# Padding the SBUF tiles of a three-stage kernel so that every tile TensorE reads begins at a multiple of 128 bytes

## The chip, the cores and the metric

The kernel runs on one core of a Trainium2 chip. The metric is device time in microseconds (us) of that core, the median of several runs. The engines are TensorE (PE, with its weight loads listed apart as PEld), VectorE (DVE), ScalarE (ACT), GpSimd (POOL) and SyncE (SP, which issues most DMAs).

## What is computed

Three layers one after the other, all in fp32. B=2 batches, S=768 positions, H=8 heads of 64, so rows of 512 numbers.

```python
# 1: retention, state decays by gamma[h] per head
state = gamma * state + outer(k[t], v[t]);  y[t] = scale * q[t] @ state
# 2: mixture of 8 experts, one expert e per row (argmax of the gate, or held from the row before)
h = relu(x @ w1[e]);  x = softmax(x @ w_gate)[e] * (h @ w2[e])      # 512 -> 1024 -> 512
# 3: 4 causal attention experts, the two with the largest gate are added
q, k, v = x @ wq[e], x @ wk[e], x @ wv[e]
a = softmax(causal(scale * q @ k.T))
out += mask[e] * w[e] * (a @ v @ wo[e])
```

## The kernel before

**Precision.** A product in fp32 is made of several faster ones: each factor is split into a high part in the type fp32r (one ACT copy) and a rest (one DVE subtraction), and three products are added in PSUM: high by high, low by high, high by low (`terms`). So nearly every matmul comes three times, with names that end in h or l, or are called `whi`/`wlo` and `hh`/`hl`.

**Stage 1** (0 to about 68 us) works through chunks of 128 positions with the tiles of the pool `s1`, and routes the rows to experts. Two `clear` DMAs (L556) write zero rows from the tile `ZR` into `x2_d` (`x_d` in the trace), the buffer into which the experts later put their rows.

**Stage 2** (about 68 to 243 us) takes the experts one after the other, sorted by their number of rows N (`CAPS`). The 64 weight pieces of 512 KB (`fetch_piece`, from `in_w_dram` into `wraw`, 5 buffers in the pool `ring`) are split into `whi` (L196, ACT) and `wlo` (L202, DVE), 10 buffers each; `prepare` keeps the splits five pieces ahead. The first layer runs over four blocks f of 2 x 128 hidden columns: for N above 224 it takes 2 x 12 matmuls of N columns (L931; the weights are stationary, the rows of the expert, x0h/x0l or xx, are the moving operand). Otherwise it takes pairs, L943 with 2N columns and L945 with N columns. Each block goes into one of three PSUM banks "B"; hh (ACT, L932) and hl (DVE, L933) read the bank and so free it. hh and hl come from the pool `mx`, whose memory is that of `s1` after stage 1. The second layer (L978; L974 for small remainders) has 512 columns: hh or hl is stationary, whi or wlo the moving operand. An indirect DMA puts the rows into `x2_d` (L1000).

**Stage 3** (about 243 to 378 us) projects q and k (L1130, 12 matmuls of 256 columns; stationary wqh, wql, wkh, wkl, moving x0h/x0l or xh/xl in turn), v with the gate logits (L1168, 12 matmuls of 260 columns; stationary x, moving wvh/wvl), makes scores (L1239), softmax (L1252 DVE, L1262 ACT, L1273 POOL), transposes (L1295), values (L1315) and the output (L1336 and, for the last group, L1363; stationary oh/ol, moving woh/wol). A flag OV decides at the end whether a slow variant must run, which it does not here.

**Order.** In stages 1 and 2 the order of each engine is written out by hand; the framework adds the semaphore waits, and it adds one wherever a tile takes memory that an earlier tile still holds. Pools give out addresses in the order of the calls, so the size of one tile moves all that follow it. Where the tiles begin, in bytes modulo 128, per partition:

| tile | before | after |
|---|---|---|
| x0h, x0l, ID, WZ, at, oh, ol | 0 | 0 |
| whi, wlo | 96 | 0 |
| hh, hl | 64 | 0 |
| xx (rows of an expert; the low half of the larger uneven experts apart) | 64 | 0 |
| wqh, wql, wkh, wkl, woh, wol | 64 | 0 |
| wvh, wvl, their four rows | 64, 80, 96, 112 and 0, 16, 32, 48 | 0 |
| ks, qh, ql, vv, xh, xl | 64 | 0 |
| blq, blk, am (stage 1) | 64 | 0 |
| gate matrix IW, its four rows | 64, 100, 8, 44 | 0 |
| xg (rows gathered for an expert) | differ | differ |

Of the kernel before, what the change touches and what calls it, by code (L numbers as in the profile page):

```python
# [32 lines left out]
RW = DM + E  # L33
E2, HD = 4, 64
# [77 lines left out]
def kernel(  # L112
# [13 lines left out]
    nc = tc.nc  # L126

    cst = ctx.enter_context(tc.tile_pool(name="cst", bufs=1))
# [16 lines left out]
    PM = cst.tile([128, E, E], F32, name="PM")  # L145
    OD = cst.tile([1, E], I32, name="OD")
    TF = cst.tile([128, 2], F32, name="TF")
    ZR = cst.tile([128, RW], F32, name="ZR")
    SH = ZR[:, :2 * E].rearrange("p (i e) -> p i e", e=E)
    WZ = cst.tile([128, 128], BF16, name="WZ")  # L150
    ONES = cst.tile([128, 128], F32, name="ONES")
    IO = cst.tile([128, CAP], BF16, name="IO")
# [14 lines left out]
    raws, pieces, ords = {}, {}, []  # L167
# [6 lines left out]
    def fetch_piece(i):  # L174
        if i >= NP:
            return
        e, r = divmod(i, 8)
        raws[i] = ring.tile([128, 1040], F32, name="wraw", bufs=RAWS)[:, :1024]
        src = w1 if r < 4 else w2
        if e:  # L180
            if e > len(ords):
                n = slice(1, 2) if e == 1 else slice(2, E)
                ords.extend(nc.values_load_multi_w_load_instructions(
                    OD[0:1, n], engines=[mybir.EngineType.SP], min_val=0, max_val=E - 1)[1])
            src = src[bass.ds(ords[e - 1], 1), r % 4].rearrange("e p n -> (e p) n")
        else:
            src = src[e, r % 4]
        parts = 1 if e else 2
        for x in range(parts):
            n = slice(x * 1024 // parts, (x + 1) * 1024 // parts)  # L190
            nc.sync.dma_start(raws[i][:, n], src[:, n])
# [23 lines left out]
                in_offset=bass.IndirectOffsetOnAxis(ap=ix[:, i], axis=0), bounds_check=T * (RW // E), oob_is_err=False)  # L215

    def first_gather():
        zi = cst.tile([128, 1], I32, name="zi")
        zo = cst.tile([128, E], F32, name="zo")
        nc.gpsimd.memset(zi, 0)  # L220
        nc.gpsimd.indirect_dma_start(
            out=zo, out_offset=None, in_=drow.rearrange("t (k e) -> (t k) e", e=E),
            in_offset=bass.IndirectOffsetOnAxis(ap=zi, axis=0), bounds_check=3 * H * C // 2 // E - 1, oob_is_err=False)
# [28 lines left out]

    with tc.tile_pool(name="s1", bufs=2) as s1:
        XB, QT, KD, QD, AM, XR, XT, LL = {}, {}, {}, {}, {}, {}, {}, {}
        N1 = NC * B

        def load_half(n, x):
# [22 lines left out]
        load_half(2, 1)  # L280
        load_half(3, 1)
        IWN = 128 + E + 1
        IW = s1.tile([128, H // 2, IWN], F32, name="IW", bufs=1)
        DT = s1.tile([128, 2, H // 2, C], F32, name="DT", bufs=1)
        XRT = s1.tile([128, B, RW], F32, name="xr", bufs=1)
        nc.gpsimd.memset(XRT[:, :, :E], 0.0)
        SB = []
        for b in range(B):
            SB.append(s1.tile([128, H // 2, D], F32, name=f"SB{b}", bufs=1))
        DN = s1.tile([128, B, NC], F32, name="DN", bufs=1)  # L290
        pS = bank("B", [128, B, H // 2, D])
        pR = bank("B", [128, 512])
        pB = bank("B", [128, 512])
# [18 lines left out]
        pI = pB[:, 2 * E:2 * E + NC]  # L312
        pOne = pR[:, 384:]
        pW8, pU = pB[:, 64:64 + E], pB[:, 64 + E:64 + 2 * E]
        W8 = s1.tile([1, E], BF16, name="W8", bufs=1)
        nc.tensor.matmul(pOne, ONB[0:1], ONB[0:1], start=True, stop=True)

        PA = {}
# [514 lines left out]
    W3, W3R = {}, {}  # L833
    W3S = (("wq", wq, [128, 4, 256]), ("wk", wk, [128, 4, 256]), ("wv", wv, [128, 4, 260]), ("wo", wo, [128, 2, 512]))

    def fetch_w3(i):
        name, src, shape = W3S[i]
        n = shape[1] * shape[2]
        W3R[i] = ring.tile([128, 1040], F32, name="wraw", bufs=RAWS)
        nc.sync.dma_start(W3R[i][:, :n], src.rearrange("p a n -> p (a n)"))  # L840

    def split_w3(i):
        name, src, shape = W3S[i]
        n = shape[1] * shape[2]
        hi = w3.tile(shape, F32R, name=name + "h")
        lo = w3.tile(shape, F32R, name=name + "l")
        rr = W3R[i][:, :n].rearrange("p (a n) -> p a n", a=shape[1])
        nc.scalar.activation(hi, rr, AF.Copy)
        nc.vector.tensor_tensor(out=lo, in0=rr, in1=hi.bitcast(F32), op=OP.subtract)
        W3[name] = (hi, lo)  # L850

    with tc.tile_pool(name="mx", bufs=2) as mp:
# [5 lines left out]
        def turn2(e, i):  # L858
            if e >= E:
                return  # L860
            if i == 0:
                XX[e] = packed(mp.tile([128, 4 * 2 * CAP], F32R, name="xx"), CAPS[e], k=4)
                XH[e], XL[e] = XX[e][:, :, 0, :], XX[e][:, :, 1, :]
                PC[e] = mp.tile([128, 2, 1 + E], F32, name="pc")
            pT = bank("A", [128, 4, 128])
            for d in range(4):
                nc.tensor.transpose(pT[:, d, :], XG[e, i][:, E + d * 128:E + (d + 1) * 128], ident)  # L867
            w = min(CAPS[e] - i * 128, 128)
            r = slice(i * 128, i * 128 + w)
            nc.scalar.activation(XH[e][:, :, r], pT[:, :, :w], AF.Copy)  # L870
            nc.vector.tensor_tensor(out=XL[e][:, :, r], in0=pT[:, :, :w], in1=XH[e][:, :, r].bitcast(F32),
                                    op=OP.subtract)
            nc.vector.tensor_tensor_reduce(out=PC[e][:, i, 1:], in0=XG[e, i][:, :E], in1=PM[:, e], scale=1.0,
                                           scalar=0.0, op0=OP.mult, op1=OP.add, accum_out=PC[e][:, i, :1])
# [22 lines left out]
        done[:] = [9, 4]  # L897
        order = ExitStack()
        order.enter_context(tc.manual_schedule(engines={ENG.PE, ENG.DVE, ENG.Activation, ENG.Pool, ENG.SP}))
        for e in range(E):  # L900
            if e == 0:
                gather(1, None)
# [161 lines left out]
    def stage3(ready=None, midway=lambda: None):  # L1064
# [21 lines left out]

        def open_group(b, g):
            if g == 0:
                LG[b] = s3.tile([128, NC, E2], F32, name="lg")
            if (b * NG + g) % 2 == 0:  # L1090
                XH3[b, g], XL3[b, g] = X0
            else:
                XH3[b, g], XL3[b, g] = (s3.tile([128, 4, GW], F32R, name=n, bufs=1) for n in ("xh3", "xl3"))
            for e in range(E2):
                QH[b, g, e] = s3.tile([128, GW], F32R, name=f"qh{e}", bufs=3)
                QL[b, g, e] = s3.tile([128, GW], F32R, name=f"ql{e}", bufs=3)
                if g == 0:
                    KS[b, e] = s3.tile([128, S], F32R, name=f"ks{e}")
# [78 lines left out]

            return evac

        TR = s3.tile([128, E2, E2], F32, name="TR", bufs=1)  # L1180
        nc.vector.tensor_tensor(out=TR, in0=cn("w4")[:, None, :].to_broadcast([128, E2, E2]),
                                in1=cn("w4")[:, :, None].to_broadcast([128, E2, E2]), op=OP.is_gt)

        def gates(b, g):
            sh = [128, GB, E2]
            l = LG[b][:, g * GB:(g + 1) * GB]
            sq = sh + [E2]
            V = nc.vector
            m = s3.tile([128, 2, GB, 1], F32, name="gm")
            q = s3.tile([128, 2] + sq[1:], F32, name="gq")  # L1190
            f = s3.tile(sh, F32, name="gf")
            ex = s3.tile(sh, F32, name="ex3")
            wt = s3.tile(sh, F32, name="wt", bufs=4)
            mine = l[:, :, :, None].to_broadcast(sq)
            others = l[:, :, None, :].to_broadcast(sq)
            yield V.tensor_reduce(out=m[:, 0], in_=l, op=OP.max, axis=AX.X)
            yield V.tensor_tensor(out=ex, in0=l, in1=m[:, 0].to_broadcast(sh), op=OP.subtract)
            yield nc.scalar.activation(ex, ex, AF.Exp)
            yield V.tensor_tensor(out=q[:, 0], in0=others, in1=mine, op=OP.is_equal)
            yield V.tensor_tensor(out=q[:, 1], in0=q[:, 0], in1=TR[:, None].to_broadcast(sq), op=OP.mult)  # L1200
            yield V.tensor_tensor(out=q[:, 0], in0=others, in1=mine, op=OP.is_gt)
            yield V.tensor_reduce(out=f, in_=q.rearrange("p k i e o -> p i e k o"), op=OP.add, axis=AX.XY)
            yield V.tensor_scalar(f, f, 1.5, None, op0=OP.is_lt)
            yield V.tensor_tensor(out=ex, in0=ex, in1=f, op=OP.mult)
            yield V.tensor_reduce(out=m[:, 1], in_=ex, op=OP.add, axis=AX.X)
            yield V.tensor_scalar(m[:, 1], m[:, 1], 1e-9, None, op0=OP.add)
            yield V.reciprocal(m[:, 1], m[:, 1])
            yield V.tensor_tensor(out=wt, in0=ex, in1=m[:, 1].to_broadcast(sh), op=OP.mult)
            WT[b, g] = wt
# [484 lines left out]
```

## Time and profile before

| | us |
|---|---|
| median of 3 runs | 385.43 (383.79 to 387.71) |
| the profiled execution | 383.58 |
| its span in the trace | 382.1 |
| its mean granted TensorE clock | 0.998 of full speed |

The profiled execution is one run, 1.85 us under the median; 1.5 us of it lie outside the span. PE is listed as busy for 98% of the span, DVE for 72%, ACT for 61%. The ends of matmuls are modelled, so that the durations of neighbouring matmuls overlap in the trace (a listed duration is longer than the distance to the next start). How fast PE really goes through a row of matmuls is therefore read from the chain that ended last, whose pieces lie end to end: its length of a piece divided by its count.

### The profile page before, as it was taken

How to read it: one execution, taken by the hardware profiler on the slowest of the kernel's cores; microseconds unless marked ns; L12 is line 12 of the kernel's file. 1: busy time of each engine (PE TensorE's matmuls, PEld its weight loads, DVE VectorE, ACT ScalarE, POOL GpSimd, SP SyncE). 2: the span in 40 equal slices, each digit the busy share in tenths (PEclk: the TensorE clock that was granted, in tenths of full speed). 3: DMA queues.
4: the chain of work that ended last, by engine and by line, in shares of the span. 5: the costliest groups of instructions: out<-in, count | busy, mean ns of one | idle time of the engine just before them, and what ended most of it. 6: DMA issues, size and time to landing. Idle time of an engine off the chain costs nothing.

```text
span 382.1 us, 8618 instructions
## 1 busy us (share of the span) xinstructions
PE 374.5 (98%) x3035; PEld 328.1 (86%) x3035; DVE 276.8 (72%) x761; ACT 233.1 (61%) x549; POOL 128.6 (34%) x177
## 2 busy tenths in 40 slices
PE   8999998999999999999999999999999999999995
PEld 3899986988979798898989798899989988988774
DVE  4568877785766778688888993368886877669762
ACT  3455573464656756677787873367776765649641
POOL 1865462063305013131310011435545342424440
PEclk9999999999999999999999999999999999999999
DMA  7999995589675767767787772141012101001212
GB/s 215 398 320 329 308 370 193 158 266 344 215 261 173 244 215 249 274 216 249 242 256 242 255 270 70 51 139 57 5 52 57 28 2 50 7 30 27 57 41 77
DMA packets 27144, 66.99 MB, mean 175 GB/s; under 512 B 5061, under 2 KB 5445, under 8 KB 27096
## 3 DMA queue, kind: packets, MB, share of 16 engines
q1 hardware_dynamic: 24402, 58.82, 47.3%
q0 software_dynamic: 2544, 7.42, 5.6%
q8 instruction: 26, 0.43, 0.5%
q14 instruction: 22, 0.18, 0.1%
q10 hardware_dynamic: 150, 0.14, 0.1%
HBM read 55.77 MB, written 11.07 MB: 175 GB/s over the span
## 4 chain that ended last, share of the span: by engine, by line
PE 87%; DMA 8%; ACT 2%; issue 1%; DVE 1%; SPq 1%; POOL 0%; ACTq 0%; POOLq 0%; DVEq 0%
PE C L978 21%; PE B L931 9%; PE C L1130 8%; PE B L943 5%; PE C L1315 5%; PE B L1295 5%; PE A L1239 4%; DMA blk<-in_blk_dram 4%; PE C L1168 4%; PE C L1336 4%; PE A L943 3%; DMA x_d<-xr 3%; PE B L945 2%; PE C L974 2%; PE C L377 2%; PE A L867 2%
## 5 line engine op out<-in xcount | busy, mean ns | idle before, releaser
L202 DVE TENSOR_TENSOR wlo<-wraw,whi 128x1024 fp32r<-128x1024 f32 x62 | 74.4, 1222 | 14.6 <-ACT whi L196 14.6
L196 ACT ACTIVATE whi<-wraw 128x1024 fp32r<-128x1024 f32 x64 | 65.7, 1051 | 4.0 <-DMA wraw<-in_w_dram 4.0
L1000 POOL DMA_INDIRECT x_d<-y,SI x16 | 19.1, 1191 | 122.8 <-ACT y L990 78.3
L1273 POOL TENSOR_SCALAR a<-a,mx,wt 128x128 f32<-128x128 f32 (+5 forms) x48 | 34.0, 716 | 49.5 <-PE A L1239 14.4
L978 PE MATMUL C<-whi,hh 128*128 128x512 f32 (+4 forms) x112 | 45.4, 406 | 0.0
L1262 ACT ACTIVATE a<-a,mx 128x128 f32<-128x128 f32 (+5 forms) x48 | 32.1, 669 | 20.7 <-DVE mx L1252 19.1
L978 PE MATMUL C<-whi,hl 128*128 128x512 f32 (+4 forms) x112 | 44.3, 395 | 0.0
L978 PE MATMUL C<-wlo,hh 128*128 128x512 f32 (+4 forms) x112 | 44.2, 395 | 0.0
L943 PE MATMUL B<-xx,whi 128*128 128x384 f32 (+3 forms) x100 | 30.9, 363 | 0.0
L1252 DVE CUSTOM_DVE_ANT_0 a<-A,MR 128x384 f32<-128x384 f32 (+3 forms) x48 | 25.4, 530 | 1.9 <-PE A L1239 1.3
L1295 PE MATMUL B<-ID,a 128*128 128x128 f32 x168 | 26.0, 274 | 0.0
L945 PE MATMUL B<-xx,wlo 128*128 128x192 f32 (+3 forms) x100 | 25.6, 256 | 0.0
L978 PEld LDWEIGHTS C<-whi,hl 128*128 128x128 f32 (+4 forms) x112 | 20.0, 179 | 6.0
L978 PEld LDWEIGHTS C<-wlo,hh 128*128 128x128 f32 (+4 forms) x112 | 20.2, 180 | 5.1
L978 PEld LDWEIGHTS C<-whi,hh 128*128 128x128 f32 (+4 forms) x112 | 20.1, 179 | 4.7
L232 POOL DMA_INDIRECT xg<-x_d,GI x14 | 17.4, 1241 | 19.8 <-DMA wraw<-in_w_dram 15.9
L917 ACT ACTIVATE hh<-t 128x128 fp32r<-128x128 f32 (+4 forms) x56 | 16.3, 318 | 12.2 <-DVE t L949 12.0
L1295 PEld LDWEIGHTS B<-ID,a 128*128 128x128 f32 x168 | 19.8, 140 | 2.4 <-issue 0.9
L1239 PE MATMUL A<-ks,qh 128*128 128x256 f32 (+3 forms) x56 | 21.5, 384 | 0.0
L1315 PE MATMUL C<-at,vv 128*64 128x256 f32 (+1 forms) x204 | 20.6, 347 | 0.0
L943 PEld LDWEIGHTS B<-xx,whi 128*128 128x128 f32 x100 | 18.7, 187 | 0.6
L945 PEld LDWEIGHTS B<-xx,wlo 128*128 128x128 f32 x100 | 19.1, 191 | 0.2
(349 smaller groups left out, 970.9 us busy)
## 6 DMA issues: line engine op xcount, KB each, us to landing
wraw<-in_w_dram SPq DMA_DIRECT2D x56, 512.0 KB, 4.3
blq<-in_blk_dram SPq DMA_DIRECT2D x16, 256.0 KB, 6.8
blk<-in_blk_dram SPq DMA_DIRECT2D x16, 256.0 KB, 6.5
wraw<-in_w_dram SPq DMA_DIRECT2D x16, 256.0 KB, 5.3
x_d<-xr SPq DMA_DIRECT2D x12, 260.0 KB, 6.3
xr<-x_d SPq DMA_DIRECT2D x10, 256.0 KB, 2.6
blq<-in_blk_dram SPq DMA_DIRECT2D x4, 512.0 KB, 6.7
blk<-in_blk_dram SPq DMA_DIRECT2D x4, 512.0 KB, 9.6
```

What stands on the lines that cost most here:

```text
L196: nc.scalar.activation(hi, raws[i], AF.Copy)
L202: eng.tensor_tensor(out=lo[:, n], in0=raws[i][:, n], in1=hi[:, n].bitcast(F32), op=OP.subtract)
L931: nc.tensor.matmul(ph[:, a, :N], w[:, k, n], x[:, k, :N], start=m == 0, stop=m == 11)
L943: nc.tensor.matmul(pa, wh[:, k, n], XX[e][:, k], start=k == 0, stop=False, skip_group_check=True)
L945: nc.tensor.matmul(pa[:, 1], wl[:, k, n], XX[e][:, k, 0], start=False, stop=k == 3, skip_group_check=True)
L978: nc.tensor.matmul(pys[i][:rows], h[:, a, n], w[:, a, :], start=f == 0 and a == 0 and m == 0, stop=f == 3 and a == 1 and m == 2)
L1130: nc.tensor.matmul(pp, w[:, k, a * 128:(a + 1) * 128], x[:, k, :], start=m == 0, stop=m == 11)
L1239: nc.tensor.matmul(ps[:, :w], qq[b, g, e][:, tq], KS[b, e][:, s0:s0 + w], start=m == 0, stop=m == 1)
L1262: nc.scalar.activation(AA[u][:, :n], AA[u][:, :n], AF.Exp, bias=mx[:, 0, i:i + 1], scale=-1.0, accum_out=mx[:, 1, i:i + 1])
L1273: nc.gpsimd.tensor_scalar(a[:, :n], a[:, :n], mx[:, 1, i:i + 1], WT[b, g][:, i, e:e + 1], op0=OP.mult, op1=OP.mult)
L1295: nc.tensor.transpose(pT[:, s - s0, :], a[:, s * C:(s + 1) * C], ident)
L1315: nc.tensor.matmul(po[j * HD:(j + 1) * HD, r], VV[b, s][:, e * HD:(e + 1) * HD], at[j][:, s, r], start=s == 0, stop=s == ns - 1, skip_grou ...
```

## The change

No instruction is added, removed or made larger; one split (wv) is written as 128x4x260 instead of 128x1040. Tiles are padded or allocated in another order so that the table above results. `ZR` (the zero rows of the clears), which had its home in the pool of constants, and the two small tiles of `first_gather` move into the pool `s1`; `SH`, which shared ZR's memory, gets a tile of its own.

```diff
-    ZR = cst.tile([128, RW], F32, name="ZR")
-    SH = ZR[:, :2 * E].rearrange("p (i e) -> p i e", e=E)
+    SH = cst.tile([128, 2, E], F32, name="SH")
+    cst.tile([128, 120], F32, name="gap")
...
-        raws[i] = ring.tile([128, 1040], F32, name="wraw", bufs=RAWS)[:, :1024]
+        raws[i] = ring.tile([128, 1056], F32, name="wraw", bufs=RAWS)[:, :1024]
...
     def first_gather():
-        zi = cst.tile([128, 1], I32, name="zi")
-        zo = cst.tile([128, E], F32, name="zo")
+        zi = s1.tile([128, 1], I32, name="zi", bufs=1)
+        zo = s1.tile([128, E], F32, name="zo", bufs=1)
...
         XB, QT, KD, QD, AM, XR, XT, LL = {}, {}, {}, {}, {}, {}, {}, {}
+        ZR = s1.tile([128, 640], F32, name="ZR", bufs=1)[:, :RW]
...
-        IW = s1.tile([128, H // 2, IWN], F32, name="IW", bufs=1)
+        IW = s1.tile([128, H // 2, 160], F32, name="IW", bufs=1)[:, :, :IWN]
...
+    W3P = {n: 288 if n == "wv" else shape[2] for n, _, shape in W3S}
+    W3T = {n: [w3.tile([128, 2 if n == "wo" else 4, W3P[n]], F32R, name=n + x) for x in "hl"]
+           for n in ("wq", "wk", "wo", "wv")}
...
-        hi = w3.tile(shape, F32R, name=name + "h")
-        lo = w3.tile(shape, F32R, name=name + "l")
+        hi, lo = (t[:, :, :shape[2]] for t in W3T[name])
...
+        ring.tile([128, 88], F32, name="end", bufs=1)
```

The other lines pad XRT, DN, W8, pc, LG, TR and gm in the same way. The code after `before` L217 lies 1 to 5 lines further down (L932 becomes L937, L978 becomes L983).

The instructions stay in their order, save for a few; their waits don't. ACT at the start of stage 2, before (x0h and hh are the rows and hidden activations of the first expert, whi the high parts of weight pieces; the names in brackets are the semaphores, DMAHW those of DMA queues, DMASW that of GpSimd's DMAs):

```order
L779 ACTIVATE x0h<-C 128x512 [waits PE_49] x2
L196 ACTIVATE whi<-wraw 128x1024 [waits DMAHW2_49]
L932 ACTIVATE hh<-B 128x512 [waits DVE_49,DMAHW6_49,PE_49,DMAHW7_49,Activation_49,Pool_49]
L196 ACTIVATE whi<-wraw 128x1024 [waits DMAHW4_49,DMAHW3_49]
L932 ACTIVATE hh<-B 128x512 [waits PE_49]
```

And ACT at the same place, now:

```order
L780 ACTIVATE x0h<-C 128x512 [waits PE_49] x2
L196 ACTIVATE whi<-wraw 128x1024 [waits DMAHW2_49]
L1645 TENSOR_LOAD OV [waits DVE_49]
L937 ACTIVATE hh<-B 128x512 [waits DMAHW4_49,DMASW0_49,DMAHW5_49,DVE_49,DMAHW6_49,PE_49,DMAHW7_49,Activation_49,Pool_49]
L196 ACTIVATE whi<-wraw 128x1024 [waits DMAHW3_49]
L937 ACTIVATE hh<-B 128x512 [waits PE_49]
```

The first hh waits for three more semaphores, DMAHW4, DMAHW5 and DMASW0, and ACT reads the flag OV ahead of it instead of after the third hh. On SP, in the changed kernel, the last two DMAs that use DMAHW4 and DMAHW5 before that are the clears:

```order
L444 DMA x_d<-PP 128x6x8 [waits DMAHW6_49,DMAHW2_49,Activation_49]
L444 DMA x_d<-PP 128x6x8 [waits DMAHW7_49,DMAHW3_49,Activation_49]
L557 DMA x_d<-ZR 128x512 [waits DMAHW4_49]
L557 DMA x_d<-ZR 128x512 [waits DMAHW5_49]
L183 TENSOR_LOAD OD [waits DVE_49]
```

They stand where they stood before. On PE, at the start of the last block of the first expert's first layer, before:

```order
L931 MATMUL B<-x0l,whi 128x256 x4
L931 MATMUL B<-x0h,whi 128x256 [waits DVE_49]
L931 MATMUL B<-x0h,whi 128x256 x3
L931 MATMUL B<-x0h,wlo 128x256 x4
L931 MATMUL B<-x0l,whi 128x256 x4
```

And now:

```order
L936 MATMUL B<-x0l,whi 128x256 x4
L1645 TENSOR_LOAD OV [waits DVE_49]
L936 MATMUL B<-x0h,whi 128x256 [waits DVE_49]
L936 MATMUL B<-x0h,whi 128x256 x3
L936 MATMUL B<-x0h,wlo 128x256 x4
```

The block's first matmul waits for DVE, as before (for the first hl, which frees the bank); PE reads OV ahead of it instead of at the start of stage 3.

## Rows read from the trace of the kernel before

**Rows 1.** The page: busy time, share of the span and instructions of each engine.
```profile
PE 374.5 (98%) x3035; PEld 328.1 (86%) x3035; DVE 276.8 (72%) x761; ACT 233.1 (61%) x549; POOL 128.6 (34%) x177
```
**Rows 2.** Stretches: busy us (count) of PE, PEld, DVE, ACT, POOL; clock, DMA share, GB/s.
```profile
90.00:243.00 153.00, 153.00 (x904) 134.12 (x903) 111.98 (x213) 98.41 (x189) 30.44 (x25) 1.00 0.68 227
201.00:223.00 22.00, 22.00 (x133) 18.68 (x132) 19.01 (x33) 17.21 (x30) 0.92 (x1) 1.00 0.75 250
250.00:345.00 95.00, 94.95 (x755) 87.13 (x754) 72.67 (x274) 63.53 (x184) 37.98 (x75) 1.00 0.13 40
378.00:380.30 2.30, 0.00 (x0) 0.00 (x0) 0.00 (x0) 0.36 (x1) 0.00 (x0) 1.00 0.69 235
380.30:382.10 1.80, 0.00 (x0) 0.00 (x0) 0.00 (x0) 0.00 (x0) 0.00 (x0) 0.50 0.06 14
```
**Rows 3.** The chain that ended last: start us, us, what; pieces of stage 2, then of stage 3.
```profile
91.94 10.87 PE B L931 x96
213.18 5.57 PE C L978 x24
218.75 11.52 PE B L931 x96
...
246.42 1.36 PE C L1130 x12
...
250.50 1.44 PE A L1168 x12
...
256.13 1.42 PE C L1130 x12
```
**Rows 4.** The same chain from 199 to 201 us, a pair of the joined first layer.
```profile
199.68 0.20 PE B L943
199.88 0.09 PE B L945
```
**Rows 5.** Timeline of PE, 59.9 to 61 us: bf16 matmuls with both operands at multiples of 128 bytes.
```profile
59.96 0.59 PE L241 MATMUL B<-WZ 128*128 128x512 bf16 x2
60.54 1.03 PE L241 MATMUL B<-WZ 128*128 128x512 bf16 x4
```
**Rows 6.** Groups by line, shapes kept apart, then groups by line.
```profile
L978 PEld LDWEIGHTS C<-whi,hh 128*128 128x128 f32 x80 | 15.1, 188 | 2.8
L1130 PE MATMUL C<-xl,wqh 128*128 128x256 f32 x24 | 3.8, 283 | 0.0
...
L978 PE MATMUL C<-wlo,hh 128*128 128x512 f32 (+4 forms) x112 | 44.2, 395 | 0.0
```
**Rows 7.** Line L1168, 250.815 to 250.82 us: one matmul on the wvl row at 0.
```profile
L1168 PE MATMUL A<-wvl,x0h x1: 277/277/277, 250.8 to 250.8; 128*128 128x260 f32 x1
```
**Rows 8.** The tile wvl, 250.3 to 251.3 us: all four rows (duration min/median/max).
```profile
L1168 PE MATMUL A<-wvl,x0h x4: 277/283/285, 250.8 to 251.2; 128*128 128x260 f32 x4
```
**Rows 9.** Line L556, the clears: issue, and time from issue to landing.
```profile
L556 SPq DMA_DIRECT2D x_d<-ZR x2: 422/524/626, 72.9 to 73.6; - x2
...
DMA to landing us min/median/max: 5.3/5.3/5.3
```
**Rows 10.** Timeline of all engines, 72 to 78 us (in brackets: idle before, and releaser).
```profile
74.60 0.60 ACT L932 ACTIVATE hh<-B 128x512 fp32r<-128x512 f32 x1 [5.38 <-DVE OV L829]
75.09 1.05 ACT L196 ACTIVATE whi<-wraw 128x1024 fp32r<-128x1024 f32 x1
75.64 0.69 DVE L933 SCALAR_TENSOR_TENSOR hl<-B,hh 128x512 fp32r<-128x512 f32 x1 [1.28 <-DMA x_d<-PP]
76.83 0.63 PE L931 MATMUL B<-x0h,whi 128*128 128x256 f32 x4
```
**Rows 11.** Timeline of PE at the end, the first and the last of six matmuls.
```profile
377.05 0.28 PE L1363 MATMUL C<-woh,oh 128*128 128x256 f32 x1
...
377.62 0.28 PE L1363 MATMUL C<-woh,ol 128*128 128x256 f32 x1
```
**Rows 12.** The tile OV: reads by the engines' sequencers (duration ns, start us).
```profile
L1640 ACTq TENSOR_LOAD <-OV x1: 467/467/467, 77.1 to 77.1; - x1
L1640 PEldq TENSOR_LOAD <-OV x1: 483/483/483, 243.4 to 243.4; - x1
```

More of the change, by code (lines that the diff above doesn't have):

```diff
@@ L244 @@
     nc.vector.memset(ONES, 1.0)
-    nc.scalar.activation(ZR[:, :1], ONES[:, :1], AF.Copy)
+    nc.scalar.activation(TF[:, :1], ONES[:, :1], AF.Copy)
     nc.vector.tensor_tensor_scan(IO, *[ONES[:, :1].to_broadcast([128, CAP])] * 2, 0.0, OP.mult, OP.add)
@@ L282 @@
         IWN = 128 + E + 1
-        IW = s1.tile([128, H // 2, IWN], F32, name="IW", bufs=1)
+        IW = s1.tile([128, H // 2, 160], F32, name="IW", bufs=1)[:, :, :IWN]
         DT = s1.tile([128, 2, H // 2, C], F32, name="DT", bufs=1)
-        XRT = s1.tile([128, B, RW], F32, name="xr", bufs=1)
+        XRT = s1.tile([128, 1056], F32, name="xr", bufs=1)[:, :B * RW].rearrange("p (b n) -> p b n", b=B)
         nc.gpsimd.memset(XRT[:, :, :E], 0.0)
@@ L289 @@
             SB.append(s1.tile([128, H // 2, D], F32, name=f"SB{b}", bufs=1))
-        DN = s1.tile([128, B, NC], F32, name="DN", bufs=1)
+        DN = s1.tile([128, 32], F32, name="DN", bufs=1)[:, :B * NC].rearrange("p (b c) -> p b c", b=B)
         pS = bank("B", [128, B, H // 2, D])
@@ L314 @@
         pW8, pU = pB[:, 64:64 + E], pB[:, 64 + E:64 + 2 * E]
-        W8 = s1.tile([1, E], BF16, name="W8", bufs=1)
+        W8 = s1.tile([1, 64], BF16, name="W8", bufs=1)[:, :E]
         nc.tensor.matmul(pOne, ONB[0:1], ONB[0:1], start=True, stop=True)
@@ L838, in fetch_w3 @@
         n = shape[1] * shape[2]
-        W3R[i] = ring.tile([128, 1040], F32, name="wraw", bufs=RAWS)
+        W3R[i] = ring.tile([128, 1056], F32, name="wraw", bufs=RAWS)
         nc.sync.dma_start(W3R[i][:, :n], src.rearrange("p a n -> p (a n)"))
@@ L863, in turn2 @@
                 XH[e], XL[e] = XX[e][:, :, 0, :], XX[e][:, :, 1, :]
-                PC[e] = mp.tile([128, 2, 1 + E], F32, name="pc")
+                PC[e] = mp.tile([128, 2, 16], F32, name="pc")[:, :, :1 + E]
             pT = bank("A", [128, 4, 128])
@@ L1088, in open_group @@
             if g == 0:
-                LG[b] = s3.tile([128, NC, E2], F32, name="lg")
+                LG[b] = s3.tile([128, 32], F32, name="lg")[:, :NC * E2].rearrange("p (t e) -> p t e", e=E2)
             if (b * NG + g) % 2 == 0:
@@ L1178, in project_v @@
             return evac
-        TR = s3.tile([128, E2, E2], F32, name="TR", bufs=1)
+        TR = s3.tile([128, 64], F32, name="TR", bufs=1)[:, :E2 * E2].rearrange("p (e o) -> p e o", e=E2)
         nc.vector.tensor_tensor(out=TR, in0=cn("w4")[:, None, :].to_broadcast([128, E2, E2]),
@@ L1188, in gates @@
             V = nc.vector
-            m = s3.tile([128, 2, GB, 1], F32, name="gm")
+            m = s3.tile([128, 16], F32, name="gm")[:, :2 * GB].rearrange("p (k g o) -> p k g o", k=2, g=GB)
             q = s3.tile([128, 2] + sq[1:], F32, name="gq")
```

## Prediction

> **What bounds the kernel now.** I read the page first: PE is listed as busy for 98% of the span, DVE for 72%, ACT for 61% [rows 1]. Then the stretches, because an average hides which stage has which limit. From 90 to 243 us, the experts after the first, PE is busy for 153.00 of 153.00 us; from 250 to 345 us, the attention, for 94.95 of 95.00 [rows 2]. DVE has 73% and 76% of these stretches to do, and 86% (19.01 of 22.00) in its busiest, 201 to 223 us. DMA runs at a share of 0.68 in the first. So the time is the number of PE's matmuls times the distance between their starts, and a change that shortens that distance shortens the kernel until DVE binds.
>
> That distance is read from the chain, whose pieces lie end to end. In stage 2 twelve pairs of 512 columns cost 5.57 us for 24, which is 232 ns each; 256 columns cost 11.52/96 = 120 ns, and 240 columns 10.87/96 = 113.2 ns [rows 3]. The granted clock there is 1.00, which is 2.4 GHz of its two levels [rows 2], so 512 columns take 213.3 ns if one column passes in each cycle, 256 take 106.7 and 240 take 100.0. Every row lies 13 to 19 ns above that. The question is how much of this excess belongs to the homes.
>
> **What the homes cost, as far as this trace shows it.** Three comparisons speak. The q and k projections are one code with two sets of moving operands: x0h/x0l at 0 modulo 128 in one group, xh/xl at 64 in the next. Twelve take 1.36 us (113.3 ns each) in the first and 1.42 us (118.3 ns) in the second [rows 3]. In the v projection the four rows of wvl lie at 0, 16, 32 and 48; the matmul on row 0 is listed with 277 ns, the four together with a median of 283 and a maximum of 285 [rows 7, 8]. And bf16 matmuls of 512 columns with both operands at 0 go at (1.03 - 0.59)/2 = 0.22 us [rows 5]; though another type, they are the nearest row for 512 columns at 0. All three have a moving operand at 0 that is faster, by 5 to 12 ns a matmul. For the stationary home the trace shows nothing by itself: L1130 with the weights at 64 and x0h at 0 is already at 113.3.
>
> What keeps 256 columns at 113.3 and 240 at 113.2 alike is not their length. A weight load is listed with 188 ns [rows 6] and there is one for each matmul; I take some 113 ns as the floor that loading sets, and so no gain where that floor is reached. The Trainium skill (TensorE: Matmul & The Clock Gate, section "LDWEIGHTS (loading the stationary operand)") puts a load at its columns over 1.2, which gives the estimate of 106.7 ns for 128. By that figure the floor would lie 6.6 ns lower, and the sum would be better by 5.4 us if padding brought PE down to it.
>
> **The change part by part.** Matmuls, where PE alone sets the end:
>
> - *512 columns.* L978 has three groups of 112, 336 matmuls [rows 6]; with 32 of L974, 60 of L1336 and 6 of L1363, by the code, that is 434. All read the moving operand at 96 or 64 now and at 0 after. Least: nothing, if this distance has another cause. Most: 232 - 213.3 = 18.7 ns each, 8.1 us. I take 218 ns, near the 0.22 us of the bf16 row: 434 x 14 ns = 6.1 us.
> - *256 and 240 columns.* L931's 192 matmuls of 256 columns (96 in each of two experts) fall from about 120 to the floor, 6 ns: 1.1 us; the 144 of L1130 on xh/xl from 118.3: 0.7 us; the 144 of L1168 from 1.44/12 = 120 [rows 3] to the row-0 pace: 0.9 us. Together 2.7 us; least nothing, most a further 5.4 us if the floor itself falls to the 106.7 ns of 256 columns (these 480, the other 144 of L1130 and the 192 of 240 columns, 816 by 6.6 ns).
> - *Joined pairs.* L943 with L945: 160 pairs of 0.29 us (0.20 + 0.09) [rows 4]; 576 columns take 240 ns. Only L943's high part has length over the floor; I take 9 ns a pair, 1.4 us; between nothing and 2.7 us (17 ns).
> - *Scores, gate matrix, stage 1 operands at 64.* By the 5 ns of L1130 for some 200 matmuls, 1.0 us; between nothing and 2 us.
>
> The sum is 11.2 us. What stage 3 gains passes only where PE is alone, nearly everywhere there; I take 0.2 us off: 11.0 us.
>
> **What it adds: a wait.** hh and hl live where the pool s1 was, and s1 now holds ZR and the tiles of the first gather. Their first writers therefore wait until the two clears have read ZR. Before, the first hh started at 74.60 us, when OV was done, and the first hl at 75.64 us, when the DMA out of PP had landed [rows 10]. The clears are issued at 72.9 and 73.6 us and land 5.3 us later, at 78.2 and 78.9 us [rows 9]. SP's order around them is the old one, so nothing makes them earlier. I take 79.1 us for the first hh: 4.5 us late. Behind it on ACT stand three splits `whi` of 1.05 us and three more hh, on DVE the first hl (0.69 us) and its splits. hl cannot end before 79.1 + 0.60 + 0.69 = 80.4 us.
>
> PE has three banks "B". The first three blocks go on; the fourth needs the bank that the first hl frees. It reached this at 76.83 us [rows 10]. So PE stands still from 76.8 to about 80.45 us, 3.65 us, and since PE later waits for nothing, that shift stays to the end. The second layer follows the fourth block 2.8 us later, when the clears have long landed; the splits that waited are caught up, since ACT has 64% and DVE 73% of the time to work. The least this wait costs is 0, if the clears' semaphore came before the hl is due (they would have to land 4 us sooner than in this trace); the most is 5 us, if the late splits hold up the second layer as well. The reads of OV (467 ns on ACT, 483 ns on PE [rows 12]) fall into this wait, and the one on PE leaves the start of stage 3; I count both as nothing. If the wait were gone, the one on PE would cost 0.5 us.
>
> An idle PE may lose its clock. At the program's end the last matmul starts at 377.62 us and lasts 0.28 [rows 11]; the clock is 1.00 until 380.3 us and 0.50 after that [rows 2], 2.4 us after the matmul. The new gap is longer, 3.65 us, so I expect 1.2 GHz for part of the fourth block: nothing if the clock holds, about 3 us if all 24 matmuls (2.8 us) take double. I take 1.5 us. The Trainium skill (the same page, section "HAM oscillation — how this bites in real kernels") describes kernels that lose the clock in each wait of PE and start the next work at the lower level; the trace's end agrees that an idle PE loses it, and no row here shows it between matmuls.
>
> Sum against the profiled execution's own 383.58 us: -11.0 + 3.65 + 1.5 = -5.85, 377.7 us. That run lay 1.85 us under the median of the runs shown, 385.43 us; the median should come to **379.6 us**.
>
> **The rivals.**
>
> - *Homes don't matter, only the wait is new* (slower). The distances of rows 3 would then come from something else, such as the load on SBUF by other engines at that moment, and the bf16 row's from its type. What speaks for it: hardly any direct row for 512 columns, which carry half of the sum, and six matmuls at the end, whose moving woh/wol lie at 64, start at 377.05 to 377.62 us [rows 11], 114 ns apart, when hardly any other engine works. Against it: the rows 7 and 8, the same line within half a microsecond. It decides if the homes give less than the 5.15 us that the gap and the clock cost; with no gain at all the time is 385.43 + 5.15 = 390.6 us. By the Trainium skill (SBUF — State Buffer, section "Specifications (TRN2)") a line of SBUF has 16 bytes; nearly all old homes are multiples of 16, so by that rule padding to 128 would bring nothing and this rival's time would come. The trace speaks against it: xh at 64, a multiple of 16, is 5 ns slower than x0h at 0.
> - *Half the gain* (no change). Only the 256-column rows behave as L1130 does, and 512 columns gain 5 ns in place of 14: 2.2 + 2.7 = 4.9 us, nearly what the wait takes: 385.43 - 4.9 + 5.15 = 385.7 us. Nothing speaks against the smaller number but the bf16 row.
> - *More gain* (faster). The stationary home counts too, and the weight load's floor falls by up to 6.6 ns: 11.0 + 5.4 - 5.15 = 11.25, 374.2 us. For it: every weight of L931, L943 and L1130 lies at 96 or 64 now. Against it: L931 with 240 columns at 113.2 and L1130 at 113.3 have different stationary homes, 96 and 64, and one pace. Clears that land early would give 385.4 - 11.0 = 374.4, the same case.
> - *DVE becomes the bound.* From 201 to 223 us it is at 86%; PE would have to be 14% faster, and by the sum above it is 4%. Priced at nothing.
>
> **How the numbers follow.** The forecast has 0.40, more gain 0.20, half the gain 0.25, homes without effect 0.15. About 1% (3.9 us) is what a measurement of this kernel can tell from no change. Faster by over 1% (under 381.6 us): the forecast and more gain, 0.60. Within 1%: half the gain, 0.25. Slower (over 389.3 us): 0.15. The range goes from 371.0 us, below the case of more gain, to 391.0 us, the case without effect; under it lies the full floor gain together with a hidden wait, over it a wait of 5 us with a full clock loss and no gain.
>
> **What would show it.** In the profile after: the chain's pieces of L983 (L978 before) at about 5.23 us for 24 and those of L936 (L931) with 256 columns at about 10.9 us for 96; the first hh at about 79.1 us, released by a DMA of the clears; a gap of some 3.7 us on PE before the fourth block, and a granted clock under 1.00 behind it. Pieces of 5.57 us would show homes without effect; L936 near 10.3 us would show a lower floor; no gap at 77 us would make the wait's term wrong; a gap with the clock at 1.00 the clock's.

## The result and the profile after

| kernel | median, us | runs | ratio to before, 95% interval |
|---|---|---|---|
| before | 384.99 | 20 | |
| after | 387.78 | 20 | 1.0066 (1.0043 to 1.0089) |
| forecast | 379.6 (371.0 to 391.0) | | 0.985 of its own 385.43 |

The change made the kernel slower by 2.8 us. The ratios compare fast executions alone, and leave out one of before that took 930.57 us. The profiled execution of after has a span of 387.1 us, 5.0 above before's 382.1; 2.6 us of that arose in stage 1, of which more below. The page, and the chain that ended last, of after (start us, us, what):

```profile
PE 376.2 (97%) x3035; PEld 331.0 (85%) x3035; DVE 276.9 (72%) x761; ACT 233.8 (60%) x549; POOL 127.6 (33%) x177
```
```profile
114.83 5.51 PE C L983 x24
...
223.60 11.50 PE B L936 x96
...
253.58 1.44 PE C L1135 x12
...
260.66 1.44 PE C L1135 x12
```

Against [rows 3]: 24 matmuls of 512 columns take 5.51 in place of 5.57 us, and not the 5.23 that the forecast asked for. 96 of 256 columns take 11.50 in place of 11.52, and not 10.9. The projections on x0 (253.58 us) take 1.44, where [rows 3] had 1.36: they became slower, and are now as slow as those on xh (260.66 us). The gain of the homes is nearly all missing.

The timeline of after at the start of stage 2, which answers to [rows 9, 10]:

```profile
76.94 1.01 SPq L557 DMA_DIRECT2D x_d<-ZR  x2
76.95 0.14 DVE L830 TENSOR_SCALAR OV<-mc 1x1 int32<-1x1 f32 x1
...
81.26 0.60 ACT L937 ACTIVATE hh<-B 128x512 fp32r<-128x512 f32 x1 [9.46 <-DMA x_d<-ZR]
81.89 0.69 DVE L938 SCALAR_TENSOR_TENSOR hl<-B,hh 128x512 fp32r<-128x512 f32 x1 [4.79 <-ACT hh L937]
...
82.64 0.74 PE L936 MATMUL B<-x0h,whi 128*128 128x256 f32 x4 [2.80 <-DVE hl L938]
```

The new wait is there as forecast: hh is released by the clears (x_d<-ZR), 4.2 us after OV is written, and PE stands still for 2.80 us until hl frees the bank (from its last modelled end; by the starts, the fourth block comes 3.2 us later after the start of stage 2 than in before).

Where PE was in each program, from the starts in the timelines (us):

| kernel | stage 2 starts | first layer of expert 0 | rest of stage 2 | stage 3 to the last matmul |
|---|---|---|---|---|
| before | 67.6 | 12.0 | 161.7 | 136.3 |
| after | 70.2 | 15.4 | 160.2 | 136.6 |
| after, second trace (e6) | 68.6 | 16.7 | 160.2 | 136.6 |
| wait alone (e3) | 68.4 | 17.5 | 161.7 | 136.5 |
| padding without wait (e2) | 68.4 | 12.3 | 161.1 | 136.8 |
| early clears (e5) | 68.5 | 12.2 | 160.2 | 136.9 |
| whi and wlo alone (e10) | 68.0 | 12.2 | 160.1 | 136.3 |
| rows 192 bytes on (e14) | 67.3 | 11.7 | 159.9 | 136.5 |

The loss is in the first layer of expert 0 (3.4 and 4.7 us in the two traces of after). Stage 2 behind it gains 1.5 us, stage 3 loses 0.4.

### The profile page after: what moved, and what is told of

It reads as the page before. It is cut to its first block, busy times and chain, and to the rows that moved or that the text cites. A ratio compares the mean times of both kernels' runs of the same rounds, so it can differ in the third digit from the quotient of the medians.

```text
span 387.1 us, 8606 instructions
## 1 busy us (share of the span) xinstructions
PE 376.2 (97%) x3035; PEld 331.0 (85%) x3035; DVE 276.9 (72%) x761; ACT 233.8 (60%) x549; POOL 127.6 (33%) x177
## 4 chain that ended last, share of the span: by engine, by line
PE 93%; DVE 3%; DMA 1%; SPq 1%; issue 1%; ACT 1%; ACTq 0%; DVEq 0%
PE C L983 20%; PE C L1135 8%; PE B L936 7%; PE B L948 5%; PE C L1320 5%; PE B L1300 5%; PE A L1244 5%; PE C L1173 4%; PE C L1341 4%; PE A L948 3%; PE C L378 3%; PE B L950 2%; PE A L329 2%; PE C L979 2%; PE C L329 2%; PE A L871 2%
## 5 line engine op out<-in xcount | busy, mean ns | idle before, releaser
L202 DVE TENSOR_TENSOR wlo<-wraw,whi 128x1024 fp32r<-128x1024 f32 x62 | 74.5, 1224 | 15.4 <-ACT whi L196 15.4
L983 PE MATMUL C<-whi,hh 128*128 128x512 f32 (+4 forms) x112 | 45.2, 404 | 0.0
L983 PE MATMUL C<-whi,hl 128*128 128x512 f32 (+4 forms) x112 | 44.0, 393 | 0.0
L983 PE MATMUL C<-wlo,hh 128*128 128x512 f32 (+4 forms) x112 | 43.8, 391 | 0.0
L983 PEld LDWEIGHTS C<-whi,hl 128*128 128x128 f32 (+4 forms) x112 | 20.0, 179 | 5.8
L983 PEld LDWEIGHTS C<-wlo,hh 128*128 128x128 f32 (+4 forms) x112 | 20.1, 180 | 4.8
L983 PEld LDWEIGHTS C<-whi,hh 128*128 128x128 f32 (+4 forms) x112 | 20.1, 179 | 4.4
L922 ACT ACTIVATE hh<-t 128x128 fp32r<-128x128 f32 (+4 forms) x56 | 16.2, 318 | 12.3 <-DVE t L954 12.0
```

What stands on the lines that cost most here:

```text
L202: eng.tensor_tensor(out=lo[:, n], in0=raws[i][:, n], in1=hi[:, n].bitcast(F32), op=OP.subtract)
L983: nc.tensor.matmul(pys[i][:rows], h[:, a, n], w[:, a, :], start=f == 0 and a == 0 and m == 0, stop=f == 3 and a == 1 and m == 2)
```

## Experiments

Theory: the wait for the clears costs what the forecast said, and the homes bring about 1 us. Rivals: the loss is the shift that after's trace shows at the end of stage 1 already (2.6 us: stage 2 starts at 70.2 in place of 67.6), or something else in ZR's new place; and the homes are worth more, at other values. The first question was the wait, the second what of the homes sets PE's pace. Paces in ns are distances from start to start, means of a row; in the maps, of its steps from the fifth on.

### The wait

**e2_const: the tiles back in the pool of constants, homes as after modulo 128.**

```diff
+    ZR = cst.tile([128, RW], F32, name="ZR")
...
-        ZR = s1.tile([128, 640], F32, name="ZR", bufs=1)[:, :RW]
...
-                     else mp.tile([128, DM], F32, name="y", bufs=4))
+                     else mp.tile([128, DM], F32, name="y", bufs=3))
```

> The changed kernel with ZR and the tiles of the first gather back in the pool of constants, all homes as in the changed kernel, and three buffers y in place of four to make room. Theory 'wait' (the wait for the clears is what made the change slower): the first hh starts within 1 us of the end of OV, PE has no gap before the fourth block, and the time is 3.4 us under the changed kernel's, 384.4 us, ratio to before 0.998. Rival (the shift of 2.6 us that stage 1 shows in the changed kernel's trace is the loss): the time stays at 387 to 388 us, ratio 1.006.

384.85 us, ratio 0.9999 (0.9973 to 1.0025). The loss is gone and the first layer of expert 0 takes 12.3 us. Padding itself brings nothing that this interval shows.

**e3_wait: the kernel before, ZR alone in s1.**

```diff
-    ZR = cst.tile([128, RW], F32, name="ZR")
...
+        ZR = s1.tile([128, 544], F32, name="ZR", bufs=1)[:, :RW]
```

> The kernel before with ZR alone moved into the pool s1; all homes as before. Theory 'wait': the first hh is released by the clears, PE stands still for about 3 us before the fourth block of the first expert, and the time is 3 to 4 us above before, ratio 1.009. Rival (the wait is caught up later, or hidden): ratio within 0.997 to 1.003.

389.93 us, ratio 1.0112 (1.0070 to 1.0155), 4.3 us. Its timeline, and its stretches (as in [rows 2]):

```profile
75.70 1.01 SPq L556 DMA_DIRECT2D x_d<-ZR  x2
...
80.09 0.60 ACT L932 ACTIVATE hh<-B 128x512 fp32r<-128x512 f32 x1 [10.10 <-DMA x_d<-ZR]
...
81.47 1.18 PE L931 MATMUL B<-x0h,whi 128*128 128x256 f32 x4 [3.63 <-DVE hl L933]
```
```profile
78.00:80.00 2.00, 0.00 (x0) 0.00 (x0) 0.00 (x0) 0.00 (x0) 0.56 (x1) 1.00 0.59 176
80.00:82.00 2.00, 0.53 (x2) 0.53 (x3) 1.03 (x2) 1.91 (x3) 1.43 (x2) 0.89 0.72 217
82.00:84.00 2.00, 2.00 (x12) 2.00 (x11) 2.00 (x3) 2.00 (x4) 1.72 (x1) 0.50 0.60 183
84.00:86.00 2.00, 2.00 (x15) 2.00 (x15) 2.00 (x3) 0.50 (x1) 1.63 (x2) 0.76 0.81 258
```

The gap is 3.63 us, and behind it the granted clock is 0.50, which is 1.2 GHz, until about 85 us: four matmuls are listed with 1.18 us in place of 0.63. The first layer takes 17.5 us, 5.5 over before: PE starts the fourth block 13.05 us into stage 2 in place of 9.19, which is 3.9, and the slow clock adds 1.6.

**e6_after: the changed kernel once more.**

> The changed kernel once more, for a second trace. Theory 'wait': a gap of 2.5 to 4 us before the fourth block, ratio 1.005 to 1.012. The 1.6 us that PE stood still in stage 1 in its first trace, with the clock at 0.50 behind it, is expected not to come again if it was an accident of that execution; if it belongs to the change, it comes again.

388.02 us, ratio 1.0085 (1.0054 to 1.0116). Its timeline, one stretch, and the same stretch of after's first trace:

```profile
80.76 1.17 PE L936 MATMUL B<-x0h,whi 128*128 128x256 f32 x4 [2.75 <-DVE hl L938]
```
```profile
82.00:84.00 2.00, 2.00 (x11) 2.00 (x11) 2.00 (x4) 1.78 (x3) 1.70 (x2) 0.50 0.67 186
```
```profile
82.00:84.00 2.00, 1.36 (x11) 1.37 (x12) 1.75 (x3) 2.00 (x3) 1.70 (x2) 1.00 0.69 162
```

The gap is 2.75 us, as in the first trace, but this time the clock fell behind it; in the first it stayed at 1.00. So the clock's term is paid in some executions and not in others. The mean granted clock of an execution is 0.995 or less in 16 of the 20 of after and in 4 of the 5 here, and in none of the 19 with the early clears below; in which place it fell, only a trace tells. In stage 1 PE waits here for 1.32 us, at another place than in the first trace and with the clock at 1.00. The first trace's wait came again, place and length, in e2_const, and there too the clock held; e3_wait and e10_w_only, whose homes are nearly all the old ones, wait for 1.07 and 1.16 us. So one program has such a wait in one execution and not in another, and the clock falls with it in one case alone; whether padding makes these waits likelier is not shown.

**e5_early and e12_early2: the clears earlier, ZR still in s1.** One line moves:

```diff
+            clear(0, GW // C)
             fetch_piece(7)
...
             send_shares(0, NC)
-            clear(0, GW // C)
```

> The changed kernel, ZR still in the pool s1, with the two clears issued some 6 us earlier (after the DMAs of xr instead of after those of PP). Theory 'wait': what hh waits for is the landing of the clears, nothing else in ZR's new place; they now land before OV is done, the first hh starts within 1.5 us of OV, PE has no gap of over 1 us before the fourth block, and the time is 3 to 4 us under the changed kernel's, ratio to before 0.995 to 1.001. Rival (another tile of s1, or the place itself, costs the time): as the changed kernel, 1.0066.

> The changed kernel with the early clears once more, beside the run with wq and wk at 64 on the same chip. If padding is worth about 1 us without the wait, ratio 0.995 to 0.999, as in its first run; a ratio over 1.000 would mean that the first run's gain was chance.

383.13 us, ratio 0.9961 (0.9942 to 0.9980), and 384.10 us, 0.9975 (0.9948 to 1.0001). The timeline of e5_early:

```profile
75.12 0.14 DVE L830 TENSOR_SCALAR OV<-mc 1x1 int32<-1x1 f32 x1
...
75.49 0.60 ACT L937 ACTIVATE hh<-B 128x512 fp32r<-128x512 f32 x1 [5.38 <-DVE OV L830]
```

hh is released by OV again, within 0.4 us, with all homes and all memory as in the changed kernel. What cost the time was the landing of the clears and nothing else in the change. Side by side with e6_after, on the same chip, e5_early takes 4.9 us less by the medians (4.6 by the means).

### The homes

**e1_map and e7_map2: the pace by itself.** In both kernels PE runs rows like this one, for pairs of homes (st, mv):

```python
for m in range(24):
    a, k = m // 4 % 2, m % 4
    nc.tensor.matmul(p[:, :n], w[:, k, a * 128:(a + 1) * 128], x[:, k], ...)
```

> This kernel leaves all three stages out: it only runs rows of 24 fp32r matmuls (256 or 512 columns, a new weight load for each) with the stationary operand at 0 (wa) or 64 (wb) modulo 128 and the moving operand at 0, 16, ... 112 (xa to xh), first with the other engines idle, then with ACT and DVE splitting weights. Theory 'distance' (what counts is where the two homes lie to each other): 256 columns take 120 ns where both are equal (wa with xa, wb with xe) and about 113 ns where they are 64 apart (wa with xe, wb with xa). Rival 'home 0' (the forecast's): wa and wb alike, and xa fastest with both. Rival 'nothing': all rows within 1 ns of each other. For 512 columns the first expects less than 3% between the rows, since 228 to 234 ns was all that the two traces show.

> Leaves all three stages out, like the first map: 13 pairs of homes (stationary, moving; 0, 4, 64 and 96 modulo 128), each visited five times in changing order, 24 matmuls a visit. Theory 'phase' (the distance between two matmuls depends on how the row is entered, not on its homes): the visits of one pair differ as much as the pairs do, 116 to 120 ns for 256 columns and 228 to 236 for 512, and homes at 4, which are no multiple of 16, take no more than these. Rival 'pair' (each pair of homes has a distance of its own): the five visits of a pair agree within 1 ns and pairs differ by 2 to 7. Rival 'lines of 16 bytes': pairs with a 4 are slower than all others by over 5%.

e1_map: with wa, xa takes 120.0 ns and xe 117.8; with wb, xa takes 117.8 and xe 118.7. So neither home 0 nor "64 apart" gave 113. The rows of 512 columns took 228 to 237 ns, the same within 1.6 ns (256 columns: 1.2) whether ACT and DVE worked or not. e7_map2: the visits of a pair agree within 1 ns in most rows, so the pace belongs in the main to the pair and not to how a row is entered. One pair has two paces: wc with xa took 113.3 to 113.4 ns in three visits and 117.8 in two, and after its first five matmuls a visit kept the one that it had. For this pair, then, the theory 'phase' is right and the entry of the row counts. Three pairs with a home at 4 varied by 1.7 to 1.8. The chain of e7_map2, first visits, in the order 256 columns (0, 0), (96, 64), (64, 0) and then 512 columns (0, 0), (64, 96), (0, 64), (0, 4):

```profile
35.56 2.88 PE B L153 x24
38.44 2.88 PE A L153 x24
41.31 2.74 PE B L153 x24
...
55.47 5.47 PE A L153 x24
60.93 5.62 PE B L153 x24
66.56 5.51 PE A L153 x24
72.06 5.75 PE B L153 x24
```

For 256 columns equal homes at 0 are as slow as the old (96, 64), and (64, 0) is the fast one, where it has its fast pace. For 512 columns (0, 0) is the fastest, 228 ns, 6 ns under (64, 96), which L978 had before. A moving home at 4 takes 240; a stationary one at 4 with the moving one at 0 takes 227 to 228. The Trainium skill (SBUF — State Buffer, section "Specifications (TRN2)") gives SBUF lines of 16 bytes, with a penalty for each crossing to a new line. The row with the moving home at 4 agrees in sign, 240 against 227 to 237; that multiples of 16 differ by 4% among themselves that rule doesn't tell.

**e4_opposite and e8_opposite2: 64 bytes apart in the kernel.**

Both are e2_const (the tiles back in the pool of constants, three buffers y) with these lines and a few alike:

```diff
+    w3.tile([128, 16], F32, name="pad3")
...
-        ring.tile([128, 88], F32, name="end", bufs=1)
+        ring.tile([128, 104], F32, name="end", bufs=1)
```

> The kernel of the run without the wait, with the weights of all three stages' fp32r products (whi, wlo, wq, wk, wv, wo) and ks at 64 modulo 128 and what they are multiplied with at 0. Theory 'distance': 624 matmuls of 256 or 260 columns fall from 120 to 113 ns, which is 4.1 us, and the time is about 380.3 us, ratio to before 0.988. Rival 'home 0': weights that leave 0 are slower, the time is that of before or above, ratio 1.00 to 1.01. Rival 'nothing': as without the wait, 0.998.

> The kernel with the homes 64 apart and no wait once more, to see whether its ratio of 0.998 (interval 0.995 to 1.001) is a gain. Theory 'phase' (homes bring at most 1 us in all): ratio 0.996 to 1.000. Rival 'distance': under 0.993.

384.81 us, 0.9978 (0.9947 to 1.0009), and 384.04 us, 0.9994 (0.9971 to 1.0017). The theory of 64 modulo 128 fell: L1130's matmuls take 117.6 ns here, and 114.7 in the kernel before, on x0, with the same homes modulo 128.

**e11_map3: is 128 the right modulus?**

> Leaves all three stages out, like the other maps: stationary and moving operand both at 0 modulo 128, the moving one at 0, 128, ... 896 bytes into its tile, three visits each. If homes modulo 128 are all that counts, every row of 256 columns takes 120.0 ns and every row of 512 takes 226.8, within 1 ns. If higher address bits count too, rows differ by 2 to 7 ns, and the three visits of one still agree.

It is not. Four pieces of the chain, 512 columns, moving operand 0, 128, 256 and 384 bytes into its tile:

```profile
68.71 5.49 PE B L152 x24
74.20 5.59 PE A L152 x24
79.79 5.46 PE B L152 x24
85.24 5.59 PE A L152 x24
```

226.6 and 233.5 ns in turn, up to 896 bytes, in each visit within 1.6 (256 columns: 119.9 and 118.7). The pace repeats every 256 bytes. With the addresses that the programs were given, the paces of all kernels then fall, but for the pairs with two paces, into one list by moving home minus stationary home, modulo 256. L978's matmuls with a full stationary operand are one example: 234.0 ns at a distance of 160 (before), 233.7 at 192 (e4_opposite), 232.8 at 128 (e2_const), 230.6 at 64 (e10_w_only, below) and 229.5 at 0 (after). It also tells why e2_const, with the homes of after modulo 128, takes 0.9 us more in stage 2 than e5_early: its hh lie 128 from whi, those of after at 0. e13_map4 tests the list.

**e13_map4: all multiples of 16.**

> Leaves all three stages out: rows of 24 matmuls with the moving operand 0, 16, ... 240 bytes past the stationary one, modulo 256 (xa to xp), each visited twice. Theory 'distance modulo 256' (the pace is set by the moving home minus the stationary home, modulo 256), with the paces that earlier runs showed: 256 columns take 120.0 ns at 0, 116.7 at 32, 117.8 at 64, 120 at 96, 118.6 at 128, about 117.4 at 160 and 113.4 at 192; 512 columns take 226.6 at 0, 233.3 at 32, 229.1 at 64, 233.6 at 96, 233.4 at 128 and 234.1 at 160. Rival (something else about the tiles): the rows of this kernel differ from these by over 2 ns.

Measured, ns a matmul (mean of two visits):

| distance | 0 | 32 | 64 | 96 | 128 | 160 | 192 | 224 |
|---|---|---|---|---|---|---|---|---|
| 256 columns | 120.0 | 117.2 | 117.8 | 120.0 | 118.7 | 117.4 | 113.4 | 118.4 |
| 512 columns | 227.2 | 233.4 | 228.9 | 233.6 | 232.9 | 234.3 | 233.4 | 233.4 |

The chain shows it for 256 columns at 176, 192 and 208:

```profile
88.83 2.86 PE A L152 x24
91.69 2.73 PE B L152 x24
94.42 2.86 PE A L152 x24
```

All the expected paces came within 1 ns of the mean (at 32 one visit took 116.8, the other 117.8). Of the odd multiples of 16, which the table leaves out, 112 is as fast as 192 for 256 columns: 113.3 ns in one visit, 115.1 in the other. At 240 the two visits of 512 columns took 226.6 and 236.5; at 48 and 208 they took 230 in e1_map and 233 to 235 here. In the kernels the last rows of 256 columns (L1363 in before), at 64, took 113.4 in before and 117.9 in e10_w_only. So some distances have two paces, and what chooses between them is not shown. The whole range is 6% for 256 columns and 4% for 512. Why the distance counts was not tried.

**e9_qk64, e10_w_only and e14_d192: the distances in the kernel.** In e9_qk64 (early clears) wq and wk lie at 64, in e10_w_only (the kernel before, with three buffers y) only whi and wlo move to 0. The edit of e10_w_only:

```diff
-        raws[i] = ring.tile([128, 1040], F32, name="wraw", bufs=RAWS)[:, :1024]
+        raws[i] = ring.tile([128, 1056], F32, name="wraw", bufs=RAWS)[:, :1024]
...
+        ring.tile([128, 88], F32, name="end", bufs=1)
```

In e14_d192 (early clears, three buffers y) the moving rows lie 192 bytes on, x0 and xx as shown, xh and xl in the same way:

```diff
+    cst.tile([128, 48], F32, name="padx")
     X0 = [cst.tile([128, 4, GW], F32R, name=n) for n in ("x0h", "x0l")]
...
-                XX[e] = packed(mp.tile([128, 4 * 2 * CAP], F32R, name="xx"), CAPS[e], k=4)
+                XX[e] = packed(mp.tile([128, 4 * 2 * CAP + 64], F32R, name="xx")[:, 48:], CAPS[e], k=4)
```

> The kernel with the early clears, and wq and wk at 64 modulo 128 in place of 0 (all else that TensorE reads stays at 0). By the pairs of the second map (moving at 0: 113.3 or 117.8 ns with the weights at 64, 120.0 with them at 0) the 288 matmuls of the q and k projections give back 2.2 to 6.7 ns each, 0.6 to 1.9 us: ratio to before 0.991 to 0.995. If homes modulo 128 decide nothing in the kernel, the ratio stays at 0.996.

> The kernel before with whi and wlo alone moved from 96 to 0 modulo 128 (no new wait, ZR where it was; three buffers y to make room). By the maps (512 columns, stationary at 64: 234 ns with the moving operand at 96, 229 with it at 0) the 368 matmuls of the second layer gain 5 ns each, 1.8 us, and the first layer changes by under 0.5 us: ratio 0.994 to 0.997. If homes decide nothing: 0.998 to 1.002.

> The kernel with the early clears, and the rows that the fp32r matmuls read (x0, xx, xh, xl) 192 bytes past a multiple of 256 in place of 0; weights, hh and oh stay at 0, so that 512 columns keep a distance of 0 and 256 columns get one of 192. Theory 'distance modulo 256': L931's 192 matmuls and L1130's 288 fall from 120.0 to about 113.5 ns, 3.1 us, L1168 by up to 0.7 us: the time is 3 to 4 us under that of the early clears (ratio 0.996 and 0.998 there), ratio to before 0.987 to 0.990. Rival (the distance is only one of several causes and does not carry over to the kernel): ratio 0.994 to 0.999.

| kernel | median, us | ratio, 95% interval |
|---|---|---|
| e9_qk64 | 383.47 | 0.9953 (0.9927 to 0.9979) |
| e10_w_only | 383.01 | 0.9940 (0.9913 to 0.9967) |
| e14_d192 | 382.95 | 0.9963 (0.9947 to 0.9979) |

All three are faster than before, by 1.4 to 2.3 us; which of them is best, and whether they beat the early clears, their intervals don't tell. e10_w_only ends at the best edge of its range, and its L978 gained 3.4 of the expected 5 ns. e9_qk64 misses its range by little, but in its trace stage 3 gains 0.4 us on the early clears, where 0.6 to 1.9 were expected. In e14_d192 the chain has the last expert's first layer at

```profile
217.13 11.05 PE B L938 x96
...
254.24 1.38 PE C L1139 x12
255.79 1.42 PE C L1139 x12
```

against 11.50 us after, 115.1 ns a matmul in place of 119.8: the distance carries over to L931. The 3 to 4 us did not come, though, and the ratio lies in the rival's range: six of the 24 rows of the projections end at 113 ns and the others at 118, the two paces of this distance in e7_map2, 117.0 in the mean, and the v projection stayed at 119. By the traces e14_d192 gains 1.2 us on the early clears, 0.35 to 0.45 in each of the first expert's first layer, the rest of stage 2 and stage 3.

## Why the prediction was wrong

**The wait** (3.65 us of gap, 1.5 of clock, forecast 5.15): right in place and mechanism, and near in price. e3_wait has it alone: 3.63 us of gap and 4.3 us (2.7 to 6.0) in the time. That the gap comes within 0.02 of the forecast is luck: the clears are issued at 75.7 and 76.3 us, 7.3 and 7.9 us after the start of stage 2 and not 5.3 and 6.0 as in before, and they land in 3.5 us and not 5.3. In after they are issued 6.7 and 7.3 us after it and land in 3.4, and the gap is 2.8 us. The slow clock cost 1.6 us in e3_wait, where it fell; that it falls in some executions only was within the bounds that were given.

**The homes** (11.0 us): this is the step that failed, the reading of three comparisons as "a moving operand at 0 that is faster". By e5_early and e12_early2 padding to 128 is worth 1.5 us (0.8 to 2.2) and 1.0 us (0 to 2.0); by e2_const, where hh lie 128 from whi, nothing that its interval shows; by the traces of before and e5_early, from the start of stage 2 on, 0.7 us. What sets the pace is the distance between the two operands, modulo 256, and at some distances how the row is entered. Term by term:

- *512 columns at 218 ns.* Mis-sized, and half of it didn't exist: the fastest pace of any pair is 226.6 ns, which is 7 ns under L978's 234 and not 14. L978's 240 matmuls with a full stationary operand fell from 234.0 to 229.5 (1.1 us in place of 3.4); its 96 with fewer columns to load stayed at 231, and so did L1336; L974's 32 fell from 234.0 to 227.8 (0.2 us). The bf16 row [rows 5] was of another type, and its 220 ns no measure for fp32r.
- *256 columns at the floor of 113 ns.* Wrong in sign. The comparison of x0 with xh in [rows 3] was real, but it showed the distance to the weights and not the home: x0 at 0 lies 192 from wq at 64, the fast distance, and xh at 128. Padding put all of them at 0, the slowest: L1130 on x0 went from 114.7 to 119.6 ns, L931 on x0 from 117.4 to 119.8, and L931 on xx stayed at 120. That the home of x0 doesn't fix the pace was to be seen in the trace before, in the chain's second visit of the same tiles and its third:

```profile
268.37 1.41 PE C L1130 x12
...
273.32 1.42 PE C L1130 x12
...
301.30 2.72 PE C L1130 x24
```

  These are x0 with wq, x0 with wk, and x0 with wq once more: 117.5, 118.3 and 113.3 ns. The first and the last have the addresses of the 113.3 in [rows 3]. They show the two paces of a distance of 192. The forecast had taken the first visit alone. It had a counter-example too: the six matmuls of [rows 11] read woh and wol at 64 and start 114 ns apart, which it put down to idle engines under the first rival; e1_map shows at most 1.6 ns between idle and busy ones, and in after these tiles lie at 0 and the line's rows of 256 columns take 119.8.
- *[rows 7, 8], v projection.* One matmul of 277 against 283 ns; with every row of wv at a multiple of 128 L1173 still takes 120 ns. The difference meant nothing: the 144 matmuls take 17.83 us in all before and 17.84 after, in place of 0.9 less.
- *Joined pairs, 1.4 us.* The first layers of the five experts with joined pairs take 47.1 us together after and 47.3 before: 0.2 us.
- *Scores, gate matrix, stage 1, 1.0 us.* Nothing to be seen: the scores take 24.57 us in all before and 24.59 in e5_early, the matmuls with the gate matrix (L412, then L413) 9.93 and 9.96, each counted from start to next start.

**The rivals.** What came is the first rival, not as it was put (homes do matter, by up to 6%), but in its balance: the gain stays under the price of the wait. Its time, 390.6, was 2.8 us too long, by the gap of 2.8 in place of 3.65, by a clock that holds in some runs, by the 1 us of gain, and by 0.4 us since the 20 executions of before have a lower median than the three. The bound of zero gain, which the forecast kept for the range, was nearer than the value it took.

## What to carry over

Before padding for alignment, look for the same pair of tiles at two places of the trace: if its pace differs there, the home alone is not what sets it. A comparison of two operands changes the distance to a third as well, so vary one home at a time in a small kernel; that takes one run. And when a tile moves into a pool whose memory is used again, each DMA that still reads it becomes a wait of the next owner: move its issue earlier with it.

## What was not expected

- PE's pace for fp32r depends on the distance of its two homes modulo 256 bytes: 113.3 to 120.0 ns for 256 columns, with 112 and 192 the fastest and 0, 80 and 96 the slowest, and 226.6 to 237 for 512, with 0 the fastest. At some distances a row falls into one of two paces (113.3 or 117.8 at 192). No one distance is best for both.
- A gap of 2.75 us took the clock to 0.50 in one execution and one of 2.80 us didn't in another, in the same place of the same kernel. In stage 1 of after's first trace PE waited only 1.58 us at a time (put down to "issue"; DMA's share was 1.05) and the clock fell to 0.50 too:

```profile
48.00:50.00 2.00, 1.06 (x17) 0.70 (x13) 1.08 (x3) 1.54 (x4) 0.09 (x1) 1.00 1.05 376
50.00:51.00 1.00, 0.35 (x4) 0.35 (x6) 0.00 (x0) 0.29 (x2) 0.69 (x1) 0.90 1.06 404
51.00:54.00 3.00, 3.00 (x28) 2.78 (x27) 1.42 (x3) 2.05 (x2) 3.00 (x3) 0.50 1.04 362
```

  This is why that trace starts stage 2 at 70.2 us, and e6_after at 68.6. In e2_const PE waits at the same place, for 1.58 us too, and the clock stays at 1.00:

```profile
50.36 0.82 PE L328 MATMUL A<-blq 64*128 64x128 f32 x9 [1.58 <-issue]
```
```profile
51.00:54.00 3.00, 3.00 (x37) 2.88 (x34) 2.89 (x5) 2.56 (x3) 2.45 (x2) 1.00 1.04 373
```

  What made the instructions late, and why the clock fell in one of the two, was not tried.
